# Attention and routed experts on one core: the leftover keys' value products as one group of four 64x64 tiles, heads swapped in half of the query tiles, queries split 256 and 320

## The chip, the core and the metric

One core of a Trainium2 chip runs one program. The metric is the device time of that program in microseconds (us). Its engines work side by side, each through its own list of instructions in order: TensorE (PE in the profile; PEld is its weight loads), VectorE (DVE), ScalarE (ACT), GpSimd (POOL) and SyncE (SP, which here only issues DMAs). Matrix products go from SBUF to PSUM, and DVE or ACT must copy them out of PSUM.

## The reference

```python
# q, k, v: 8 batches x 8 heads x 576 x 64, float32
scores = 1/sqrt(64) * q @ k.T
keep   = scores >= max(scores, -1) - tau
attn   = exp(scores - max) where keep, else 0;  attn /= sum(attn) + 1e-9
x      = (attn @ v), heads side by side           # 4608 x 512
logits = x @ w_gate                               # 4608 x 8, the router
# all 36864 (token, expert) pairs in descending order; a token goes to the first expert
# that still has room (576 tokens each); then per expert
out    = max(x @ w1[e], 0) @ w2[e]
```

## The kernel before

The first half of the program is attention (`attention`), the second the router and the experts (`moe`). The change is in attention and in the host's layout of q, k and v (`lay_qk`, `lay_v`).

**Pairs, tiles and slots.** Attention goes through 32 pairs of heads (pair p is batch p//4, heads 2j and 2j+1 with j = p%4). A pair has nine query tiles: tiles 0 to 7 are 128 queries of one head each (even ones the first head, odd ones the second), and tile 8 holds the last 64 queries of both heads, one head in each half of the partitions. There are 288 tiles, and the main loop (`for s_ in range(...)`) takes two of them per turn, in four steps that belong to different tiles. I call a turn a slot; a pair has 4.5 slots. In a slot PE writes the scores of two tiles into two `sc` tiles (`score`); DVE reads each `sc`, scales it into `z` and finds the maximum (`mx`); ACT takes the exponential of `z` into `pp` (tiles 0 to 7) or `pm` (tile 8) (`ex`); DVE applies the threshold and sums for the two tiles of the slot before (`stt`); PE transposes the weights of two older tiles into a `tb` bank (`tr`), and ACT copies the `tb` of the slot before into `pt` (`trev`). There are two `sc` tiles, one pair of `tb` banks and two `xo` banks in PSUM.

**Keys: 512 and 64 left over.** The 576 keys are four blocks of 128 and 64 left over. The four blocks are transposed by `tr`. For the left over, the first head's last 64 keys and the second head's first 64 keys lie side by side in memory (a `pp` tile holds both heads, 2 x 576 wide), so that one transposition of 128 columns takes both: `left` writes them into unused columns of the two `sc` tiles of that slot, and `leftev` has ACT copy them into `pl`. For tile 8 the second head's keys are stored rolled by 64 (`ke`), so that its leftover columns are in the same place as the first head's, and POOL copies 64 columns of `pm` once more.

**The value products.** `pv_unit(p,f,u)` multiplies key block u with queries of half f (288 each) for both heads: two matmuls of 128 rows and 64 columns side by side in the array. I call it a unit. Four units fill a bank `xo`; `pl_unit(p,f)` adds the leftover keys, again as two matmuls of 128 rows and 64 columns: 128 rows of `pl` hold both heads' leftover keys, and the values of the other head are stored as zeros. Then ACT copies `xo` into `xt`. So a pair has eight `pv` units and two `pl` units.

**Order.** Nothing is reordered at run time: the Python loop sets each engine's list. Units wait in `queue`, and `columns` takes as many per slot as `credit` allows (`RATE` is added per slot: two values, the second while work of the finished batch waits in `aux`). What a unit leaves to be copied out is put into `later` and written at the next `flush`. The slot writes in this order: scores and leftover transpositions on PE; `flush`; the `pt` copies; `flush`; `leftev`; `mx`, `ex`, `stt`; units; `aux` work (`whole`: gate logits `lg_unit`, their transposes, rows of x); transposes. In a slot in which `leftev` is due the first `flush` is left out. One rule breaks this order, because there are two `pt` buffers:

```python
while i==0 and p>1 and (p-2,"pv") not in have: st["credit"]=9; columns(); flush()
```

It stands ahead of the `pt` copy of a pair's tile 0. If the pair two before has not had its last unit, that unit is written now, on PE, and its copies to `xt` on ACT. For even p, tile 8 of pair p and tile 0 of pair p+1 are in one slot.

The slot with `leftev` is the one that the prediction speaks of: I call it the leftover slot; there is one per pair. In it the next `z` must wait for `leftev`, because the transposed leftover keys stand in the bank of `sc` that `z` reads.

Of the kernel before, what the change touches and what calls it, by code (L numbers as in the profile page):

```python
# [18 lines left out]
S=576; D=64; HS=288; QK=3*HS+2*S  # L19
PPB=8; LTB=1; VTB=5; HOLD=1; CAPV=3.3; XW=520; RATE=(2.4,2.4); NBO=2; NDEF=4; XTB=4; XTY=1.05; XT0=2.0; XRB=2  # L20


def attention(ctx, tc, qk, vl, tau, wgd, xrows, xts, Lg, nb_batches, ident, swap, R, after_first):
# [14 lines left out]
    def load(p):  # L38
        b,j=divmod(p,4)
        x=ld.tile([128,QK],F32,name="qk"); v=ld.tile([128,5,128],F32,name="vt",bufs=VTB)  # L40
        if p==0:

            a=HS+128; h=HS+S
            for q,c,e in ((nc.sync,0,a),(nc.scalar,h,h+a),(nc.sync,a,h),(nc.scalar,h+a,2*h),(nc.sync,2*h,QK)):
# [5 lines left out]
        for n,w in ((("k",0),HS),(("q",0),S),(("k",1),HS),(("q",1),S),(("ke",1),HS)):  # L50
            t[n]=x[:,c:c+w]; c+=w
        t["ke",0]=t["k",0]
        LD[p]=t
# [7 lines left out]
    def score(t):  # L61

        p,i=divmod(t,9); kd=LD[p]
        sc=ps_s.tile([128,2,512],F32,name="sc"); SC[t]=sc
        if i<8: todo=((i%2,"k",slice(0,128),slice(i//2*128,i//2*128+128)),)
        else: todo=((0,"ke",slice(0,64),slice(512,576)),(1,"ke",slice(64,128),slice(512,576)))
        for h,k,o,c in todo:
            for f in range(2):
                r=slice(64*f,64*f+64)
                T.matmul(sc[o,f,:HS], kd["q",h][r,c], kd[k,h][r,:],start=True,stop=True)  # L70
    ZB={}
    def mx(t):
        nb=wk.tile([128,2],F32,name="nb",bufs=6); NBI[t]=nb
        z=wk.tile([128,2,HS],F32,name="z",bufs=5); ZB[t]=z
        V.tensor_scalar(z,SC.pop(t)[:,:,:HS],-0.125,None,op0=ALU.mult,op1=ALU.min,accum_out=nb[:,0:1])  # L75
        G.tensor_scalar(nb[:,1:2],nb[:,0:1],taub[:,0:1],None,op0=ALU.add)  # L76
    def pview(t):
        p,i=divmod(t,9)
        if i==8:
            if t not in PB: PB[t]=wk.tile([128,S+D],F32,name="pm")  # L80
            return PB[t][:,:S]
        k=(p,i//2)
        if k not in PB: PB[k]=wk.tile([128,2,S],F32,name="pp",bufs=PPB)
        return PB[k][:,i%2]
    def ex(t):
        A.activation(pview(t),ZB[t].rearrange("p a b -> p (a b)"),AF.Exp,bias=NBI[t][:,0:1],scale=-1.0)  # L86
# [10 lines left out]
    def turn(o,x):  # L97
        for r in range(2):
            g=slice(64*r,64*r+64); T.transpose(o[:,r],x[g],ident[g,g])  # L99
# [4 lines left out]
    def tr(t,first):  # L104
        p,i=divmod(t,9)
        tb=bank(t,first)
        pv=pview(t)
        o=64 if (i<8 and i%2) else 0
        for kb in range(4): turn(tb[:,:,kb],pv[:,o+kb*128:o+(kb+1)*128])
# [8 lines left out]
    def left(p,n,t):  # L118
        sc=SC[t] if t is not None else ps_s.tile([128,2,512],F32,name="sc")
        LB[p,n]=sc  # L120
        for g in ((0,1,2),(3,))[n]: turn(sc[:,:,HS+64*(g%3):HS+64*(g%3)+64],PB[p,g].rearrange("p a b -> p (a b)")[:,512:640])
        if n: turn(sc[:,:,HS+64:HS+128],PB[p*9+8][:,512:640])
    def leftev(p):
        a=LB.pop((p,0)); b=LB.pop((p,1))
        A.activation(PL[p][:,0:384].rearrange("p (g r q) -> p r g q",g=3,r=2),a[:,:,HS:HS+192].rearrange("p r (g q) -> p r g q",g=3),AF.Copy)  # L125
        A.activation(PL[p][:,384:512].rearrange("p (r q) -> p r q",r=2),b[:,:,HS:HS+64],AF.Copy)
        for r in range(2): A.activation(PL[p][64*r:64*r+64,512:576],b[64*r:64*r+64,r,HS+64:HS+128],AF.Copy)
# [10 lines left out]
    def pv_unit(p,f,u):  # L138
        b,j=divmod(p,4)
        if b not in XT: XT[b]=wk.tile([128,4,S],F32,name="xt",bufs=XTB)  # L140
        if u==0: XO[p,f]=bank_v([128,512])
        xo=XO[p,f]; q=slice(f*HS,(f+1)*HS); v=LD[p]["v"]
        for h in range(2):
            T.matmul(xo[64*h:64*h+64,:HS],v[:,u,64*h:64*h+64],PT[p][:,h,u,q],start=(u==0),stop=False,skip_group_check=True)  # L144
    def pl_unit(p,f):
        b,j=divmod(p,4)
        q=slice(f*HS,(f+1)*HS); xo=XO.pop((p,f))
        for h in range(2):
            T.matmul(xo[64*h:64*h+64,:HS],LD[p]["v"][:,4,64*h:64*h+64],PL[p][:,q],start=False,stop=True,skip_group_check=True)  # L149
        if f==1: have[p,"pv"]=1  # L150
        return VB[id(xo)],lambda: A.activation(XT[b][:,j,q],xo[:,:HS],AF.Copy)  # L151
# [10 lines left out]
    def rd_unit(b):  # L162
        rd=RD[b]
        ps=bank_g(b,[128,512])
        T.matmul(ps[:,:4],swap,rd[:,:,8],start=True,stop=True)
        rm=wk.tile([128,4,2],F32,name="rm",bufs=XTB+NBO); RD["m",b]=rm
        def ev():
            V.tensor_copy(rm[0:64,:,0],rd[0:64,:,8]); V.tensor_copy(rm[64:128,:,1],rd[64:128,:,8])
            V.tensor_copy(rm[0:64,:,1],ps[0:64,:4]); V.tensor_copy(rm[64:128,:,0],ps[64:128,:4])
        return ev  # L170
    LT={}
    def lg_unit(b,f):
        if f==0: LT[b]=wk.tile([128,S+D],F32,name="lt",bufs=LTB)
        ps=bank_g(b,[128,512])
        for j in range(4):
            T.matmul(ps[32*j:32*j+32,:HS],wg[:,j],XT[b][:,j,f*HS:(f+1)*HS],start=True,stop=True,tile_position=(0,32*j))
        def ev():
            A.activation(LT[b][:,f*HS:(f+1)*HS],ps[:,:HS],AF.Copy)
            if f==1: G.tensor_scalar(LT[b][:,S:],LT[b][:,S-D:S],1.0,0.0,op0=ALU.mult,op1=ALU.add)
        return ev  # L180
# [42 lines left out]
    queue=[]; aux=[]; later=[]; late=[]; late2=[]; st={"last":-9,"slot":0,"credit":0.0}  # L223
    def push_pair(p):
        b,j=divmod(p,4)
        def when(n): return lambda: have.get((p,n),1<<30)+HOLD<=st["slot"]
        if p==NP-1:


            def left(f):  # L230
                k,g=pl_unit(p,f); g(); k[0]=True
# [3 lines left out]
            for g in (lambda: rd_unit(b)(),lambda: left(0),lambda: left(1),lambda: lg_unit(b,0)(),lambda: lg_unit(b,1)(),lambda: lgt_unit(b)(),lambda: lgm_unit(b)()):  # L235
                queue.append(("n",when("pl"),False,g))
            queue.append(("n",lambda: not later,False,lambda: late.extend([lambda c=c: xt_unit(b,c) for c in range(5)])))
            return
        for f in range(2):
            for u in range(4): queue.append(("c",when("t5" if f==0 else "t8"),u==0,lambda f=f,u=u: pv_unit(p,f,u)))  # L240
            if (f,j)==(0,3): queue.append(("n",when("t8"),False,lambda: rd_calc(b)))
            queue.append(("c",when("pl"),False,lambda f=f: pl_unit(p,f)))
# [3 lines left out]
    def finish(b):  # L246
        aux.extend([(0,lambda: rd_unit(b)),(0,lambda: lg_unit(b,0)),(0,lambda: lg_unit(b,1)),(1,lambda: lgt_unit(b)),(0,lambda: lgm_unit(b))])
# [8 lines left out]
    def columns():  # L256
        while queue and queue[0][1]():
            if queue[0][0]=="c":
                if st["credit"]<1 or (queue[0][2] and not free_v()): return
                st["credit"]-=1  # L260
            c,_,_,g=queue.pop(0); r=g()
            if c=="c" and r:
                later.append(r)
                if aux: return
    def whole():
        n=0
        while n<2 and aux and not XO and free_v() and st["slot"]>=st["last"]+aux[0][0]:
            r=aux.pop(0)[1](); n+=1; st["last"]=st["slot"]
# [11 lines left out]
    for s_ in range(-2,NT//2+2):  # L280
# [15 lines left out]
        for t in ev_:  # L296
            p,i=divmod(t,9)
            if i==5: push_pair(p)
# [582 lines left out]
def lay_qk(q,k):  # L881
# [3 lines left out]
    q=np.transpose(q,(0,1,3,2)); k=np.transpose(k,(0,1,3,2)); e=np.roll(k,-64,-1)  # L885
    for j in range(4):
        for f in range(2):
# [4 lines left out]
            o[:,j,f,:,c:]=e[:,2*j+1,:,f*HS:f*HS+HS]  # L892
    return o.reshape(B,4,128,QK)

def lay_v(v):


    B=v.shape[0]; o=np.zeros((B,4,128,5,128),v.dtype)
    for j in range(4):
        for h,o0 in ((0,0),(1,64)):  # L900
            o[:,j,:,0:4,64*h:64*h+64]=v[:,2*j+h,o0:o0+512].reshape(B,4,128,64).transpose(0,2,1,3)
        o[:,j,0:64,4,0:64]=v[:,2*j,512:576]; o[:,j,64:128,4,64:128]=v[:,2*j+1,0:64]
    return o
# [44 lines left out]
```

## Time and profile before

| | us |
|---|---|
| median of 3 runs (lowest, highest) | 1008.64 (1008.61, 1010.94) |
| the profiled execution: its time | 1010.9 |
| its span, first to last instruction | 1009.1 |
| attention, about | 5 to 487 |
| DVE busy between 20 and 480 | 430.38 of 460 |
| PE busy between 20 and 480 | 450.78 of 460 |
| ACT busy between 20 and 480 | 396.88 of 460 |

The time is some 2 us more than the span in the profiled execution, and that execution is the slow one of the three. In the rows of the profile `L75` is the `z` of `mx`, `L90` is `stt`, `L86` the exponential, `L70` the scores, `L99` all transposes inside attention (`tb` those of `tr`, `sc` those of `left`), `L114` and `L116` the `pt` copies, `L125` to `L127` `leftev`, `L144` the `pv` units, `L149` the `pl` units and `L151` their copies into `xt`. A PE instruction of this program is half of a float32 matmul, so a unit of two matmuls is four rows of the trace ("x4"). Instruction lengths overlap: a row's length is more than the distance to the next start.

### The profile page before, as it was taken

The page shows a single profiled execution, that of the slowest core. Times are in us where ns is not written, and L with a number is a line of the kernel's source. Part 1 is how long each engine was busy: PE and PEld are TensorE (multiplying, and loading weights), DVE is VectorE, ACT ScalarE, POOL GpSimd, SP SyncE. Part 2 cuts the span into 40 slices and gives each one's busy share as a digit, 9 for nine tenths or more (in the row PEclk, how much of TensorE's full clock was granted, in tenths as well). Part 3 has the DMA queues.
Part 4 walks back from the last instruction along what each step waited for, and adds up shares of the span by engine and source line. Part 5 has one row for each costly group of instructions (what it writes and reads, how often), then busy time and mean ns, then how long its engine had stood idle before and what let it go on. Part 6 is the DMA issues. An engine that isn't in the chain of part 4 may idle for free.

```text
span 1009.1 us, 24058 instructions
## 1 busy us (share of the span) xinstructions
PE 973.7 (96%) x9141; PEld 715.7 (71%) x9141; DVE 782.2 (78%) x2154; ACT 636.1 (63%) x1257; POOL 269.3 (27%) x443
## 2 busy tenths in 40 slices
PE   7999999999999999999879999999999999999996
PEld 4555555655655555555669789797887979899894
DVE  7999999999999999999578888788687787525220
ACT  6888888888888888888644344254342534545340
POOL 3333433333433343332020221212221203220202
PEclk9999999999999999999978999999999999999998
DMA  6322143243432133110771433434343415341101
GB/s 230 108 79 88 56 152 118 87 155 125 157 109 104 61 109 109 61 51 27 267 238 67 140 128 107 148 100 145 120 133 120 148 62 171 110 152 54 41 11 42
DMA packets 36004, 113.33 MB, mean 112 GB/s; under 512 B 4400, under 2 KB 5168, under 8 KB 35376
## 3 DMA queue, kind: packets, MB, share of 16 engines
q1 hardware_dynamic: 28496, 89.18, 25.1%
q0 software_dynamic: 5888, 19.03, 6.0%
q10 hardware_dynamic: 1504, 3.59, 1.1%
q8 instruction: 72, 1.18, 0.5%
q14 instruction: 44, 0.36, 0.1%
HBM read 89.34 MB, written 21.38 MB: 110 GB/s over the span
## 4 chain that ended last, share of the span: by engine, by line
PE 58%; DVE 19%; ACT 10%; issue 9%; DMA 2%; DVEq 0%; POOLq 0%; ACTq 0%
PE pf L781 21%; PE pf L813 19%; DVE z L75 7%; DVE pp L90 7%; ACT pp L86 5%; PE xo L144 5%; PE sc L70 4%; PE tb L99 3%; ACT pt L114 2%; PE pt L726 2%; ACT pt L116 1%; PE xo L205 1%; PE rps L434 1%; PE xo L149 1%; ACT pl L125 1%
## 5 line engine op out<-in xcount | busy, mean ns | idle before, releaser
L75 DVE TENSOR_SCALAR_CACHE_REDUCE z<-sc 128x576 f32<-128x576 f32 x288 | 205.8, 750 | 32.7 <-ACT pl L125 24.7
L76 POOL TENSOR_SCALAR nb<-nb,taub 128x1 f32<-128x1 f32 x288 | 146.5, 509 | 289.5 <-DVE z L75 255.9
L86 ACT ACTIVATE pp<-z,nb 128x576 f32<-128x576 f32 x256 | 187.7, 774 | 53.2 <-DVE z L75 52.5
L90 DVE SCALAR_TENSOR_TENSOR pp<-z,nb,pp 128x576 f32<-128x576 f32 x256 | 199.9, 812 | 0.3
L813 PE MATMUL pf<-w2h,H 128*128 128x512 f32 x576 | 195.1, 402 | 0.7 <-DVE H L366 0.7
L70 PE MATMUL sc<-qk 64*128 64x288 f32 (+1 forms) x1280 | 189.0, 432 | 2.6 <-DVE z L75 2.3
L144 PE MATMUL xo<-pt,vt 128*64 128x288 f32 x1024 | 151.7, 418 | 6.1 <-ACT xt L151 4.7
L114 ACT ACTIVATE pt<-tb 128x512 f32<-128x512 f32 x256 | 139.4, 591 | 8.8 <-PE tb L99 7.3
L813 PE MATMUL pf<-w2l,H 128*128 128x512 f32 x320 | 128.3, 401 | 0.0
L820 POOL DMA_INDIRECT out_dram<-y,idx x40 | 43.5, 1087 | 308.5 <-ACT y L816 248.9
L813 PEld LDWEIGHTS pf<-w2h,H 128*128 128x128 f32 x576 | 106.5, 189 | 20.0 <-DVE H L366 1.6
L70 PEld LDWEIGHTS sc<-qk 64*128 64x128 f32 (+1 forms) x1280 | 92.2, 180 | 30.2 <-DVE z L75 12.3
L144 PEld LDWEIGHTS xo<-pt,vt 128*64 128x64 f32 x1024 | 62.7, 136 | 70.3 <-issue 28.1
L99 PEld LDWEIGHTS tb<-ident,pp 64*128 64x128 f32 x2048 | 75.6, 139 | 50.9 <-issue 23.3
L781 PE MATMUL pf<-xh,w1h 128*128 128x288 f32 (+2 forms) x512 | 111.0, 303 | 0.7 <-ACT xh L727 0.7
L781 PE MATMUL pf<-xh,w1l 128*128 128x288 f32 (+2 forms) x512 | 110.6, 302 | 0.0
L781 PE MATMUL pf<-xl,w1h 128*128 128x288 f32 (+2 forms) x512 | 110.6, 302 | 0.0
L816 ACT ACTIVATE y<-pf 128x512 f32<-128x512 f32 x40 | 23.9, 598 | 127.0 <-PE pf L813 123.6
L99 PE MATMUL tb<-ident,pp 64*128 64x64 f32 x2048 | 94.3, 229 | 3.4 <-ACT pt L114 3.1
L793 ACT ACTIVATE hf<-pf 128x576 f32<-128x576 f32 x56 | 36.5, 653 | 89.5 <-PE pf L781 84.9
L781 PEld LDWEIGHTS pf<-xh,w1h 128*128 128x128 f32 x512 | 82.8, 192 | 1.5 <-ACT xh L727 1.1
L781 PEld LDWEIGHTS pf<-xh,w1l 128*128 128x128 f32 x512 | 82.6, 191 | 0.2
(199 smaller groups left out, 1358.4 us busy)
## 6 DMA issues: line engine op xcount, KB each, us to landing
qk<-qk_dram SPq DMA_DIRECT2D x31, 1008.0 KB, 5.0
w2s<-w_dram SPq DMA_DIRECT2D x32, 512.0 KB, 4.7
w1s<-w_dram SPq DMA_DIRECT2D x28, 512.0 KB, 5.2
vt<-vl_dram SPq DMA_DIRECT2D x32, 320.0 KB, 5.4
xrows<-pp SPq DMA_DIRECT2D x24, 260.0 KB, 2.3
xts<-xt SPq DMA_DIRECT2D x2, 1152.0 KB, 5.3
pt<-xts SPq DMA_DIRECT2D x2, 1152.0 KB, 7.5
xrows<-xr SPq DMA_DIRECT2D x8, 260.0 KB, 2.3
```

The source lines that it names most:

```text
L70: T.matmul(sc[o,f,:HS], kd["q",h][r,c], kd[k,h][r,:],start=True,stop=True)
L75: V.tensor_scalar(z,SC.pop(t)[:,:,:HS],-0.125,None,op0=ALU.mult,op1=ALU.min,accum_out=nb[:,0:1])
L76: G.tensor_scalar(nb[:,1:2],nb[:,0:1],taub[:,0:1],None,op0=ALU.add)
L86: A.activation(pview(t),ZB[t].rearrange("p a b -> p (a b)"),AF.Exp,bias=NBI[t][:,0:1],scale=-1.0)
L90: V.scalar_tensor_tensor(pv,ZB.pop(t).rearrange("p a b -> p (a b)"),NBI[t][:,1:2],pv,op0=ALU.is_le,op1=ALU.mult,accum_out=den_of(p)[:,p%4, ...
L99: g=slice(64*r,64*r+64); T.transpose(o[:,r],x[g],ident[g,g])
L114: A.activation(PT[p][:,i%2,:,(i//2)*128:(i//2+1)*128].rearrange("p k (r q) -> p r k q",r=2),tb,AF.Copy)
L144: T.matmul(xo[64*h:64*h+64,:HS],v[:,u,64*h:64*h+64],PT[p][:,h,u,q],start=(u==0),stop=False,skip_group_check=True)
L781: T.matmul(ps[:,h,:n],s[w][:,k,f*128:(f+1)*128],s[x][:,k,cols[h]],start=(i==0),stop=(i==11))
L793: A.activation(hf,ps[:,:,:HS],AF.Relu)
L813: T.matmul(ps[:,0,:],H[:,f,c:c+128],s[w][:,f],start=(f==0 and j==0),stop=e)
L820: G.indirect_dma_start(out=out,out_offset=IOA(ap=s["idx"][:n,t:t+1],axis=0),in_=y[:n],in_offset=None)
```

## The change

Per pair the leftover keys become one group. Queries are halved 256 and 320 (`FQ`) instead of 288 and 288. In query tiles 0 to 3 the first head's weights lie first in memory, as before; in tiles 4 to 7 the two heads change places (`place`), so that there the second head's last 64 keys and the first head's first 64 keys are left over. Then, for the two halves of the queries, the four products (head, half) use four different quarters of the array, each 64 rows by 64 columns, without the zeros. They are written one behind the other in one `pl_unit`, which therefore comes once a pair, when both `xo` banks are full; both banks stay open until then, and both copies to `xt` go into `later` together.

```diff
-S=576; D=64; HS=288; QK=3*HS+2*S
-PPB=8; LTB=1; VTB=5; ... RATE=(2.4,2.4); ...
+S=576; D=64; HS=288; QK=2*HS+2*S; FQ=(slice(0,256),slice(256,576))
+PPB=8; LTB=1; VTB=4; ... RATE=(2.02,2.6); ...
...
+    def place(i): return i%2 if i<4 else 1-i%2
+    PM=[cst.tile([128,S+2*D],F32,name="pm%d"%n) for n in range(2)]
+    for m in PM: V.memset(m[:,:D],0.0); V.memset(m[:,D+S:],0.0)
...
-        if i==8: G.tensor_scalar(PB[t][:,S:],PB[t][:,S-D:S],1.0,0.0,op0=ALU.mult,op1=ALU.add)
...
-    def pl_unit(p,f):
-        b,j=divmod(p,4)
-        q=slice(f*HS,(f+1)*HS); xo=XO.pop((p,f))
-        for h in range(2):
-            T.matmul(xo[64*h:64*h+64,:HS],LD[p]["v"][:,4,64*h:64*h+64],PL[p][:,q],start=False,stop=True,skip_group_check=True)
-        if f==1: have[p,"pv"]=1
-        return VB[id(xo)],lambda: A.activation(XT[b][:,j,q],xo[:,:HS],AF.Copy)
+    def pl_unit(p,fs=(0,1)):
+        b,j=divmod(p,4); r=[]
+        for f in fs:
+            xo=XO.pop((p,f)); q=FQ[f]; n=q.stop-q.start
+            for a in range(2):
+                g=slice(64*a,64*a+64); h=a^f
+                T.matmul(xo[64*h:64*h+64,:n],LD[p]["v"][g,f,512:576],PL[p][g,q],start=False,stop=True,skip_group_check=True)
+            r.append((VB[id(xo)],lambda xo=xo,q=q,n=n: A.activation(XT[b][:,j,q],xo[:,:n],AF.Copy)))
+        have[p,"pv"]=1
+        return r
...
-            for u in range(4): queue.append(("c",when("t5" if f==0 else "t8"),u==0,lambda f=f,u=u: pv_unit(p,f,u)))
+            for u in range(4): queue.append(("c",when("t3" if f==0 else "t8"),u==0,lambda f=f,u=u: pv_unit(p,f,u)))
...
-            queue.append(("c",when("pl"),False,lambda f=f: pl_unit(p,f)))
+        queue.append(("c",when("pl"),False,lambda: pl_unit(p)))
...
-                if st["credit"]<1 or (queue[0][2] and not free_v()): return
+                if st["credit"]<1 or (queue[0][2] and (not free_v() or (aux and not XO and st["held"]!=st["open"] and st["slot"]<NT//2))):
+                    return
```

What goes with it: the rolled keys `ke` are gone (`qk` per pair 864 KB instead of 1008), the values are stored once per half of the queries (`vt` 576 KB instead of 320, four buffers instead of five); tile 8 has two lasting buffers `pm0` and `pm1` with 64 zero columns at either end instead of POOL's copy; the reciprocals of tile 8 are swapped by a small matmul in the first gate unit's bank instead of in a bank of their own (`rd_unit` goes into `lg_unit`); the last pair keeps two separate `pl` groups. The experts are not touched. In the changed file the lines of attention are numbered a little differently: `z` is L74, the `pt` copies L113 and L115, `leftev` L124 to L126, `pv` L143, `pl` L151, the `xt` copies L152, transposes L98 and scores L69.

Two places of the lists, both in the leftover slot of pair 26 (the pairs 16, 18, 22 and 30 have the same). First ACT, before, from the `pt` copy of tile 8 (`L116`) on:

```order
L116 ACTIVATE pt<-tb 128x8x64
L114 ACTIVATE pt<-tb 128x2x4x64
L125 ACTIVATE pl<-sc 128x2x3x64
L126 ACTIVATE pl<-sc 128x128
L127 ACTIVATE pl<-sc 64x64 x2
L86 ACTIVATE pp<-z,nb 128x576 x2
```

The two `pt` copies are followed at once by `leftev`. The same place after the change:

```order
L115 ACTIVATE pt<-tb 128x8x64
L152 ACTIVATE xt<-xo 128x256
L152 ACTIVATE xt<-xo 128x320
L113 ACTIVATE pt<-tb 128x2x4x64
L124 ACTIVATE pl<-sc 128x2x3x64
L125 ACTIVATE pl<-sc 128x128
L126 ACTIVATE pl<-sc 64x64 x2
L86 ACTIVATE pp<-z,nb 128x576 x2
```

Both copies of the pair before (pair 25 of the list, whose `pt` buffer is wanted) now stand between the two `pt` copies, ahead of `leftev`. PE in the same slot, before, from the transposes of tile 8 on (`tb<-ident,pm`):

```order
L99 MATMUL tb<-ident,pm 128x64 x8
L99 MATMUL tb<-ident,pp 128x64 x8
L70 MATMUL sc<-qk 128x288 x2
L99 MATMUL sc<-ident,pp 128x64 x6
L70 MATMUL sc<-qk 128x288 x2
L99 MATMUL sc<-ident,pp 128x64 x2
L99 MATMUL sc<-ident,pm 128x64 x2
L144 MATMUL xo<-pt,vt 64x288 x4
L99 MATMUL tb<-ident,pp 128x64 x16
```

After two score tiles, each with its leftover transposes, come two units of the value products. After the change:

```order
L98 MATMUL tb<-ident,pm_100 128x64 x8
L98 MATMUL tb<-ident,pp 128x64 x8
L69 MATMUL sc<-qk 128x288 x2
L98 MATMUL sc<-ident,pp 128x64 x6
L69 MATMUL sc<-qk 128x288 x2
L98 MATMUL sc<-ident,pp 128x64 x2
L98 MATMUL sc<-ident,pm_100 128x64 x2
L143 MATMUL xo<-pt,vt 64x320 x2
L151 MATMUL xo<-pl,vt 64x256 x2
L151 MATMUL xo<-pl,vt 64x320 x2
L143 MATMUL xo<-pt,vt 64x256 x6
L98 MATMUL tb<-ident,pp 128x64 x16
```

The last unit and the leftover group of the pair before, whose copies ACT writes ahead of `leftev`, stand here behind all score tiles and leftover transposes of the slot.

More of the change, by code (lines that the diff above doesn't have):

```diff
@@ L107, in tr @@
         pv=pview(t)
-        o=64 if (i<8 and i%2) else 0
-        for kb in range(4): turn(tb[:,:,kb],pv[:,o+kb*128:o+(kb+1)*128])
+        o=(64,0) if i==8 else (64*place(i),)*2
+        for kb in range(4): turn(tb[:,:,kb],*(pv[:,c+kb*128:c+(kb+1)*128] for c in o))
     def trev(t):
@@ L217, in xt_unit @@
         return ev
-    queue=[]; aux=[]; later=[]; late=[]; late2=[]; st={"last":-9,"slot":0,"credit":0.0}
+    queue=[]; aux=[]; later=[]; late=[]; late2=[]; st={"last":-9,"slot":0,"credit":0.0,"held":-1,"open":0}
     def push_pair(p):
```

88 lines of the change are left out of this document (42 added, 46 removed).

## The prediction

> **What bounds attention.** First the busy time of each engine between 20 and 480 us (columns: PE, PEld, DVE, ACT, POOL; clock, DMA share, GB/s), then the waits on DVE in that stretch (us in total, times, longest).
>
> ```profile
> 20.00:480.00 460.00, 450.78 (x5265) 265.07 (x5267) 430.38 (x1233) 396.88 (x766) 164.29 (x330) 1.00 0.28 98
> ```
>
> ```profile
> DVE z L75 <- ACT pl L125: 24.7, 30, 1.3
> DVE z L75 <- PE sc L70: 1.8, 4, 1.0
> ```
>
> By busy time PE (98%) is the engine in demand, DVE (94%) comes next. But DVE loses 29.6 us, and 24.7 of them in 30 waits of one kind: `z` waits for the first copy of `leftev`. It hardly ever waits for PE. The DVE timeline shows the beat (start, length, engine, line):
>
> ```profile
> 202.55 0.76 DVE L75 TENSOR_SCALAR_CACHE_REDUCE z<-sc 128x576 f32<-128x576 f32 x1 [0.72 <-ACT pl L125]
> ...
> 205.40 0.75 DVE L75 TENSOR_SCALAR_CACHE_REDUCE z<-sc 128x576 f32<-128x576 f32 x1
> ...
> 375.57 0.75 DVE L75 TENSOR_SCALAR_CACHE_REDUCE z<-sc 128x576 f32<-128x576 f32 x1
> ...
> 376.25 0.75 DVE L75 TENSOR_SCALAR_CACHE_REDUCE z<-sc 128x576 f32<-128x576 f32 x1
> ...
> 379.20 0.76 DVE L75 TENSOR_SCALAR_CACHE_REDUCE z<-sc 128x576 f32<-128x576 f32 x1 [0.72 <-ACT pl L125]
> ...
> 422.41 0.76 DVE L75 TENSOR_SCALAR_CACHE_REDUCE z<-sc 128x576 f32<-128x576 f32 x1 [1.02 <-ACT pl L125]
> ...
> 451.43 0.76 DVE L75 TENSOR_SCALAR_CACHE_REDUCE z<-sc 128x576 f32<-128x576 f32 x1 [1.32 <-ACT pl L125]
> ```
>
> From the first `z` of a slot to the first of the next it is 2.85 us (202.55 to 205.40): two `z` and two `stt` without a gap. Into a leftover slot it is 3.63 (375.57 to 379.20). The wait there has three sizes, 0.72, 1.02 and 1.32: with none, one and two copies out of `xo` ahead of `leftev` in ACT's list, 0.30 each. So the quantity to forecast is what stands ahead of `leftev` on ACT, and when it can run. The slot that ends at 379.20, on ACT and on PE:
>
> ```profile
> 376.36 1.45 ACT L86 ACTIVATE pp<-z,nb 128x576 f32<-128x576 f32 x2
> 377.72 0.58 ACT L116 ACTIVATE pt<-tb 128x512 f32<-128x512 f32 x1
> 378.20 0.59 ACT L114 ACTIVATE pt<-tb 128x512 f32<-128x512 f32 x1
> 378.68 0.49 ACT L125 ACTIVATE pl<-sc 128x384 f32<-128x384 f32 x1
> ```
>
> ```profile
> 377.74 0.70 PE L70 MATMUL sc<-qk 64*128 64x288 f32 x4
> 378.27 0.22 PE L99 MATMUL sc<-ident,pp 64*128 64x64 f32 x2
> 378.33 0.23 PE L99 MATMUL sc<-ident,pm 64*128 64x64 f32 x2
> 378.49 1.19 PE L144 MATMUL xo<-pt,vt 128*64 128x288 f32 x8
> ```
>
> ACT runs without a break: exponentials, two `pt` copies 0.48 apart, `leftev`; `z` follows 0.52 after `leftev` starts. PE is not in this chain: it comes to its value products at 378.49, 2.92 after the slot's first `z`, and nobody waits for them.
>
> **Leftover slots after the change.** I count from the two lists what lies ahead of `leftev` in the 31 leftover slots that a `z` follows. Now: in 13 nothing; in 8 two `xt` copies behind both `pt` copies, of products that PE wrote a slot earlier; in 1 two gate copies; in 9 (pairs 8, 10, 12, 14, 16, 18, 22, 26, 30) the two `xt` copies between the `pt` copies, of a leftover group that PE is given only in this slot, behind all scores and leftover transposes. The first three kinds have prices above: 13 x 0.72 = 9.4, 9 x 1.32 = 11.9.
>
> The nine forced ones are new: ACT, and behind it `leftev` and `z`, waits for PE. No row shows this, so I build it. PE can start the group where it now starts the units, 2.92 after the slot's first `z`. Its own length, and how soon ACT follows:
>
> ```profile
> 203.38 1.39 PE L70 MATMUL sc<-qk 64*128 64x288 f32 x12
> 204.71 0.71 PE L149 MATMUL xo<-pl,vt 128*64 128x288 f32 x4
> 205.34 0.66 PE L205 MATMUL xo<-ident,xt 128*128 128x128 f32 x4
> ...
> 208.05 1.68 PE L144 MATMUL xo<-pt,vt 128*64 128x288 f32 x12 [0.34 <-ACT xt L151]
> ...
> 210.21 1.19 PE L70 MATMUL sc<-qk 64*128 64x288 f32 x8
> 211.33 0.71 PE L144 MATMUL xo<-pt,vt 128*64 128x288 f32 x4
> ```
>
> ```profile
> 482.09 1.19 PE L149 MATMUL xo<-pl,vt 128*64 128x288 f32 x8
> ```
>
> ```profile
> 482.85 0.90 ACT L151 ACTIVATE xt<-xo 128x288 f32<-128x288 f32 x2 [3.05 <-PE xo L149]
> ```
>
> A unit of 288 columns adds 0.49 (x8 1.19 in the next fence, x12 1.68), by columns 0.43 for 256 and 0.54 for 320; alone it takes 0.63 until the next work starts (204.71 to 205.34), so a run of another shape costs 0.14 to 0.15. The x12 at 203.38 holds four matmuls of 64x64 for tile 8 in place of two of 64x128: 1.33 to the next start against 1.12 for the plain x8, 0.21 more for the changes of shape and nothing more for four quarters at once. So the new group should take 0.54, and 0.76 from start to result (0.71 for 288); ACT follows 0.05 later (482.09 + 0.71 = 482.80, 482.85). Then from the slot's first `z`: 2.92 + 0.76 + 0.05 = 3.73; two copies 0.60 and one `pt` copy 0.48 bring `leftev` to 4.81 and `z` to 5.33, against 3.63: 1.70 more, a wait of 2.42. So in the four slots where the group stands first (pairs 8 to 14). In the other five a unit of 320 stands ahead of it, with a change of shape: 0.54 + 0.15 = 0.69 more, a wait of 3.11. Together 4 x 2.42 + 5 x 3.11 = 25.2.
>
> The ends of the 2.92: the second score tile cannot start before the second `z` has read its bank (376.25 + 0.75 = 377.00), and from that tile to the units it is 0.75 (377.74 to 378.49): 2.18. On the other side a slot in which PE was behind:
>
> ```profile
> 405.44 0.75 DVE L75 TENSOR_SCALAR_CACHE_REDUCE z<-sc 128x576 f32<-128x576 f32 x1
> ```
>
> ```profile
> 408.93 1.19 PE L144 MATMUL xo<-pt,vt 128*64 128x288 f32 x8
> ```
>
> That is 3.49. I take the middle row, 2.92; the ends move nine slots by -0.74 or +0.57: -6.7 or +5.1.
>
> **Sum of the leftover slots:** 9.4 + 11.9 + 25.2 = 46.5, less 24.7 now: +21.8 us. DVE has no free time to give it back: in the other slots it runs without a gap.
>
> **The other parts.** PE: per pair two `pl` units of 0.49 become one group of 0.54, 31 x 0.44 = 13.6 saved; changes of shape fall from 379 to 369 by my count, 1.5 more. This PE time is off the path; it can only take away the 1.8 us that `z` waits for scores. I take -1.5; slots with three units of 320 columns (1.62 against 1.46) could put some back. The gain of 0 elsewhere is covered by DVE's 2.85 per slot, and without that cover it would be 15. Opening a bank: both are open until the group, so the next pair's first unit waits for an `xt` copy (0.34 at 208.05 before); nobody but the transposes stands behind it. POOL loses 32 small copies, at 36% busy. DMA: 1440 KB a pair instead of 1328 at a share of 0.28, through SP's list in unchanged order and asked for more than a slot ahead: 0 (it would be the extra 112 KB, under 1 us a pair at the 98 GB/s of this stretch, if nothing covered it). The start:
>
> ```profile
> 1.59 0.11 DVE L271 MEMSET idle<- 128x64 uint32 x1
> ```
>
> ```profile
> 1.76 2.10 PE L278 MATMUL xo<-idle 128*128 128x128 bf16 x18 [1.76 <-DVE idle L271]
> 4.08 2.29 PE L70 MATMUL sc<-qk 64*128 64x288 f32 x8 [0.22 <-DMA qk<-qk_dram]
> ```
>
> Four fills of zeros at 0.11 stand ahead of the one that the warm-up matmuls need; these end 0.22 ahead of the first scores, so 0.44 - 0.22 = 0.2. The end (last pair: same columns, two groups of two quarters, one change of shape more) I take as 0.1. The experts are unchanged and move along whole.
>
> Sum: 21.8 - 1.5 + 0.3 = +20.6, call it +20. The profiled execution took 1010.9, so it would take 1031; it is 2.3 above the median. Against the median: 1008.6 + 20 = **1028.6 us**. Its own range: -6.7 and -2 for stalls that also vanish gives 1020; +5.1 and +2 for the long slots gives 1036.
>
> **Rivals.** (a) *PE is the bound, and the saving counts.* For it: 98% busy, four quarters at once. Then 1008.6 - 15.1 = 993.5. Against it: waits of DVE for PE are 1.8 us in all, and slots without `leftev` are exactly DVE's length. It decides only if the beat of 2.85 were set by PE. By the Trainium skill, "TensorEngine Tiling (Array Packing)", section "Theoretical Speedup", a dimension of at most 64 brings a factor of 2, so halved leftover products (0.97 to 0.49 a pair) would give 31 x 0.48 = 14.9 us, about the same time; the x12 row agrees on the factor. By the skill's "Perfetto Trace Analysis", section "Identifying the Most-Contended Engine", matmul busy time is no measure of how close PE is to its limit, and for VectorE busy time is a fair one: by that rule DVE's 94% counts and (a) falls. Chance 0.05.
>
> (b) *ACT's waits shrink, a little faster.* If the forced copies came off their place (the group done before ACT has finished the first `pt` copy, 2.63 after the first `z`) and all leftover slots cost 0.72: 31 x 0.72 = 22.3, less 24.7, less 1.8: -4, 1004.5. The sign changes where the nine forced slots cost under (24.7 + 1.2 - 9.4 - 11.9) / 9 = 0.5 each. Against it: the earliest group ends at 2.18 + 0.76 = 2.94. Chance 0.05.
>
> (c) *The forced slots cost no more than two copies,* 9 x 1.32 = 11.9 in place of 25.2: +6.7, 1015. It would need PE to run ahead of the second `z`, which only another bank of `sc` would allow. Chance 0.09.
>
> (d) *The change does not do what it says on PE:* the four quarters run one after the other or in two pairs. Then every group takes 0.5 to 1.6 longer, which counts in the nine slots: 5 to 14 more, 1034 to 1043. Against it: the x12 row. Chance 0.06.
>
> **Chances.** The forecast has 0.75, of which 0.03 lie above 1036. Range 1014 to 1036: it leaves out (a), (b), most of (d) and that edge, about 0.18. Changes within 0.3% (3 us), about what a measurement of this kernel can tell from none, come from (b) and the gap between (b) and (c): 0.04. Faster 0.07, slower 0.89.
>
> **What would show it.** In the profile of the changed kernel: the wait of `z` for L124 at some 45 us, in nine slots above 2 us, the five later ones longest; ACT idle ahead of L152 for PE in those nine; slots without `leftev` still at 2.85; PE's time on L151 about half of L149's, with more idle time on PE; the experts' length unchanged. The forecast is wrong if the nine slots show L152 ready when ACT comes to it, or if slots of 2.85 become shorter.

## The result and the profile after

The changed kernel takes 1026.69 us (median of 4 runs, 1025.84 to 1028.29) against 1008.77 for the kernel before in the same comparison (4 runs, 1008.61 to 1010.94): a ratio of 1.0174, 95% interval 1.0155 to 1.0194. It is slower, and the forecast of 1028.6 lies 1.9 above the time. The profiled execution took 1026.09, its span is 1024.3.

First the busy time of each engine between 20 and 480 us (columns as before: PE, PEld, DVE, ACT, POOL; clock, DMA share, GB/s), then the waits of DVE and of ACT between 20 and 490 us (us in total, times, longest).

```profile
20.00:480.00 460.00, 427.13 (x5063) 246.59 (x5061) 415.31 (x1193) 381.24 (x736) 150.23 (x292) 1.00 0.30 103
```

```profile
DVE z L74 <- ACT pl L124: 45.1, 31, 3.5
```

```profile
ACT xt L152 <- PE xo L151: 10.8, 9, 1.4
```

PE has 23.7 us less to do in this stretch than before, since it does less work per pair and gets through fewer pairs, and DVE, which had 430.38, has 415.31: it stands still for longer. Nearly all of its idle time is one wait, `z` for the first copy of `leftev`: 45.1 us instead of 24.7. The wait of `z` for scores (1.8 before) is gone. And ACT now waits nine times for the leftover group on PE ahead of an `xt` copy, which it did only once before, for the last pair (3.05 at 482.85). The difference is 20.4 - 1.8 = 18.6 us; from the third slot's first `z` to the last slot's, the trace shows 18.3. Before, on DVE:

```profile
11.77 0.75 DVE L75 TENSOR_SCALAR_CACHE_REDUCE z<-sc 128x576 f32<-128x576 f32 x1
...
470.64 0.75 DVE L75 TENSOR_SCALAR_CACHE_REDUCE z<-sc 128x576 f32<-128x576 f32 x1
```

After, with the ends of a leftover slot of the cheap kind (406.05) and of a forced one (424.86) between:

```profile
10.74 0.75 DVE L74 TENSOR_SCALAR_CACHE_REDUCE z<-sc 128x576 f32<-128x576 f32 x1
...
406.05 0.76 DVE L74 TENSOR_SCALAR_CACHE_REDUCE z<-sc 128x576 f32<-128x576 f32 x1 [0.72 <-ACT pl L124]
...
419.26 0.75 DVE L74 TENSOR_SCALAR_CACHE_REDUCE z<-sc 128x576 f32<-128x576 f32 x1
...
424.86 0.76 DVE L74 TENSOR_SCALAR_CACHE_REDUCE z<-sc 128x576 f32<-128x576 f32 x1 [2.69 <-ACT pl L124]
...
487.91 0.75 DVE L74 TENSOR_SCALAR_CACHE_REDUCE z<-sc 128x576 f32<-128x576 f32 x1
```

470.64 - 11.77 = 458.9 before, 487.91 - 10.74 = 477.2 after. I call this stretch the loop time; it holds nothing of the start or of the experts. DVE is busy for 430.29 of the 458.87 and for 429.79 of the 477.16: its work in the loop is the same, and the whole difference is time in which it stands still. The slot from 419.26 to 424.86 is the one whose lists stand under the change (pair 26). ACT and PE in it:

```profile
420.05 1.45 ACT L86 ACTIVATE pp<-z,nb 128x576 f32<-128x576 f32 x2 [0.41 <-DVE z L74]
421.41 0.58 ACT L115 ACTIVATE pt<-tb 128x512 f32<-128x512 f32 x1
423.24 0.71 ACT L152 ACTIVATE xt<-xo 128x256 f32<-128x256 f32 x2 [1.25 <-PE xo L151]
423.84 0.60 ACT L113 ACTIVATE pt<-tb 128x512 f32<-128x512 f32 x1
424.32 0.51 ACT L124 ACTIVATE pl<-sc 128x384 f32<-128x384 f32 x1
```

```profile
421.70 0.23 PE L98 MATMUL sc<-ident,pm 64*128 64x64 f32 x2
421.86 0.76 PE L143 MATMUL xo<-pt,vt 128*64 128x320 f32 x4
422.55 0.77 PE L151 MATMUL xo<-pl,vt 64*64 64x256 f32 x8
```

Read from right to left: `z` starts 0.54 after `leftev`; `leftev` stands behind a `pt` copy (0.48) and two `xt` copies (0.60); these wait 1.25 for PE, which does the unit of 320 and the group only behind all scores and transposes of the slot. Eight rows of the group run in 0.77, where four rows of one old `pl` unit took 0.71: the four quarters do work side by side. To the next start on PE a group takes 0.70 to 0.77, the two old units of a pair 0.54 to 0.71 each, some 1.2 together.

### The profile page after: what moved, and what is told of

The parts are those of the page before. It is cut to its first block, busy times and chain, and to the rows that moved or that the text cites. A ratio compares the mean times of both kernels' runs of the same rounds, so it can differ in the third digit from the quotient of the medians.

```text
span 1024.3 us, 24024 instructions
## 1 busy us (share of the span) xinstructions
PE 962.7 (94%) x9141; PEld 703.2 (69%) x9141; DVE 781.3 (76%) x2158; ACT 633.5 (62%) x1257; POOL 259.5 (25%) x411
## 4 chain that ended last, share of the span: by engine, by line
PE 62%; DVE 15%; ACT 11%; issue 9%; DMA 2%; DVEq 0%; POOL 0%; POOLq 0%; ACTq 0%
PE pf L781 21%; PE pf L813 18%; PE xo L143 7%; DVE z L74 6%; PE sc L69 5%; DVE pp L90 5%; ACT pp L86 4%; PE tb L98 3%; ACT pt L113 3%; ACT xt L152 2%; PE pt L726 2%; ACT pl L124 1%; PE rps L434 1%; ACT pt L115 1%; PE xo L204 1%
## 5 line engine op out<-in xcount | busy, mean ns | idle before, releaser
L74 DVE TENSOR_SCALAR_CACHE_REDUCE z<-sc 128x576 f32<-128x576 f32 x288 | 205.4, 749 | 49.9 <-ACT pl L124 45.1
L75 POOL TENSOR_SCALAR nb<-nb,taub 128x1 f32<-128x1 f32 x288 | 150.7, 523 | 325.4 <-DVE z L74 294.9
L69 PE MATMUL sc<-qk 64*128 64x288 f32 (+1 forms) x1280 | 190.6, 432 | 5.2 <-DVE z L74 5.1
L143 PE MATMUL xo<-pt,vt 128*64 128x320 f32 (+1 forms) x1024 | 148.4, 416 | 15.9 <-DVE xr L212 5.4
L113 ACT ACTIVATE pt<-tb 128x512 f32<-128x512 f32 x256 | 139.0, 590 | 2.2 <-PE tb L98 1.9
L143 PEld LDWEIGHTS xo<-pt,vt 128*64 128x64 f32 x1024 | 64.7, 136 | 82.7 <-issue 31.0
L98 PEld LDWEIGHTS tb<-ident,pp 64*128 64x128 f32 x2048 | 75.0, 138 | 63.3 <-ACT pt L113 34.9
L69 PEld LDWEIGHTS sc<-qk 64*128 64x128 f32 (+1 forms) x1280 | 88.6, 177 | 38.3 <-DVE z L74 26.3
L98 PE MATMUL tb<-ident,pp 64*128 64x64 f32 x2048 | 94.0, 229 | 7.9 <-ACT pt L113 7.4
```

The costliest lines, as they stand in the source:

```text
L69: T.matmul(sc[o,f,:HS], kd["q",h][r,c], kd["k",h][r,:],start=True,stop=True)
L98: g=slice(64*r,64*r+64); T.transpose(o[:,r],x[r%len(x)][g],ident[g,g])
L113: A.activation(PT[p][:,i%2,:,(i//2)*128:(i//2+1)*128].rearrange("p k (r q) -> p r k q",r=2),tb,AF.Copy)
L143: T.matmul(xo[64*h:64*h+64,:q.stop-q.start],v[:,f,128*u+64*h:128*u+64*h+64],PT[p][:,h,u,q],start=(u==0),stop=False,skip_group_check=True)
```

## The experiments

Twelve kernels ran, on four chips on which the kernel before took 1013.7 to 1015.7; so times are compared as ratios to it, each taken on one chip, with the loop time of the profiled execution beside them. The two need not agree to better than some 4 us (run 4: 1.2% less is 12 us, and its loop time is 8.0 less): the rest of the span, start and experts, varies from 547 to 558 us between these profiles. In the loop DVE is busy for 427 to 431 us in every run but run 11 (435), so loop times differ by how long DVE stands still. "Forced" is a leftover slot in which the rule for the `pt` buffers puts `xt` copies between the two `pt` copies, by the lists.

| run | edit | ratio, 95% interval | loop time | to before |
|---|---|---|---|---|
| - | before | 1 | 458.9 | 0 |
| - | the change | 1.0174 (1.0155 to 1.0194) | 477.2 | +18.3 |
| 1 | change, `xt` copies behind `leftev` | 1.0137 (1.0108 to 1.0166) | 474.7 | +15.8 |
| 2 | change, only units forced | 1.0103 (1.0076 to 1.0130) | 470.3 | +11.4 |
| 3 | before, `xt` copies behind `leftev` | 1.0009 (0.9993 to 1.0025) | 462.0 | +3.1 |
| 4 | change, RATE (2.2,3.0) | 0.9880 (0.9848 to 0.9913) | 450.9 | -8.0 |
| 5 | change, RATE (2.2,2.6) | 1.0083 (1.0053 to 1.0113) | 470.6 | +11.7 |
| 6 | run 4, group twice | 1.0020 (1.0000 to 1.0040) | 462.9 | +4.0 |
| 7 | change, two groups, RATE (2.4,2.4) | 1.0004 (0.9986 to 1.0023) | 462.0 | +3.1 |
| 8 | before, RATE (2.0,2.0) | 1.0122 (1.0089 to 1.0154) | 470.2 | +11.3 |
| 9 | change, group twice | 1.0232 (1.0193 to 1.0271) | 481.6 | +22.7 |
| 10 | before, RATE (2.4,3.0) | 1.0044 (1.0025 to 1.0064) | 462.8 | +3.9 |
| 11 | run 4, `leftev` split | 1.0149 (1.0116 to 1.0182) | 474.5 | +15.6 |
| 12 | change, RATE (2.02,3.0) | 0.9954 (0.9936 to 0.9971) | 455.7 | -3.2 |

**Runs 1 and 3: only the place of the copies on ACT.** In a leftover slot all `xt` copies are written behind `leftev`, in the changed kernel and in the one before.

```diff
-            while i==0 and p>1 and (p-2,"pv") not in have: st["credit"]=9; columns(); flush()
+            while i==0 and p>1 and (p-2,"pv") not in have:
+                st["credit"]=9; columns()
+                if (p-2,"pv") not in have: flush()
             trev(t); have[p,f"t{i}"]=s_
-        flush()
+        if not p8 or ev_[-1]==NT-1: flush()
...
-            if i==8: leftev(p); have[p,"pl"]=s_
+            if i==8:
+                leftev(p); have[p,"pl"]=s_
+                flush()
```

> The changed kernel, with one thing moved: in a leftover slot the copies out of xo are written on ACT behind leftev, where the changed kernel writes them between or behind the two pt copies. PE's list stays as it is, the nine forced groups too. Theory (the nine forced slots cost because leftev, and with it the next z, stands on ACT behind two copies that wait for PE): the waits of z for L124 fall from 45.1 us to 26 x 0.72 + 5 x 1.5 = 26, the five being pairs 16, 18, 22, 26 and 30, where a pt copy must itself still wait for a unit of 320 on PE; so 19 us less, 1026.7 - 19 = 1008 (1005 to 1011). Rival A (PE is late by the group itself, or PE's work is the bound): PE's list has not changed, so the time stays at 1026.7. Rival B (the copies are merely moved and cost the same 0.60 behind leftev, since ACT has no free time): 9 x 0.6 + 10 x 0.6 come back one slot later, about 1015 to 1020.

> The kernel before with the same move as the first run: copies out of xo in a leftover slot are written behind leftev. Theory: its 22 copies ahead of leftev cost it what lies above 0.72 in its waits: 24.7 - 31 x 0.72 = 2.4 us, so 1006.4 (1005 to 1008). Rival (ACT's full list gives it back in the next slot): 1008.8.

Both expectations of my theory failed. The waits behind `leftev` fall, by 13 us (I had expected 19) and by 6 us, but most or all of it comes back. Waits of DVE in run 1, then in run 3:

```profile
DVE z L74 <- ACT pl L124: 32.1, 30, 1.6
DVE z L74 <- PE sc L69: 8.1, 17, 1.7
```

```profile
DVE z L75 <- ACT pl L125: 19.0, 28, 0.8
DVE z L75 <- PE sc L70: 9.5, 13, 1.0
```

The new wait for scores has its cause on PE. In run 1, the group of a forced slot, and what stands behind it on PE; then DVE in the next slot:

```profile
297.15 0.77 PE L151 MATMUL xo<-pl,vt 64*64 64x256 f32 x8
299.25 1.52 PE L143 MATMUL xo<-pt,vt 128*64 128x256 f32 x12 [1.33 <-ACT xt L152]
```

```profile
302.01 0.76 DVE L74 TENSOR_SCALAR_CACHE_REDUCE z<-sc 128x576 f32<-128x576 f32 x1 [0.74 <-PE sc L69]
```

The copies are also what frees the `xo` banks. Moved behind `leftev`, they hold up the next pair's first unit (1.33 here, 0.36 at the same kind of place in the changed kernel), and the transposes and the scores of the next slot stand behind that unit on PE. In all PE waits 23.3 us for `L152` in run 1 against 12.8 in the changed kernel. For run 1, rival B, which gave the copies back one slot later, came nearest, and yet no outcome that I had named was right: its 1015 to 1020 is a ratio of 1.006 to 1.011, and 1.0137 lies between that and the unchanged time. For run 3 the rival, nothing gained, was right. Their reason, ACT's full list, is not what the trace shows. So of the 18 us that the change loses, moving the copies on ACT alone gives back 2.5.

**Run 2: no forced group, only forced units.**

```diff
-            while i==0 and p>1 and (p-2,"pv") not in have: st["credit"]=9; columns(); flush()
+            c0=st["credit"]
+            while i==0 and p>1 and (p-2,"u") not in have: st["credit"]=1; columns()
+            st["credit"]=c0
```

(`have[p,"u"]` is set with the last `pv` unit, and `pl` is claimed in `leftev`.)

> The changed kernel with the rule's condition loosened: ahead of tile 0 only the units that read the pt buffer are forced (the last unit of 320), not the group of leftover keys, which reads pl; pl is claimed only in leftev. Copies out of xo stay where the changed kernel has them, but none is forced between the pt copies any more: 29 leftover slots have no copy ahead of leftev, 3 have two. Theory (the forced copies on ACT): 24 x 0.72 + 5 x 1.5 (a pt copy still waits for the forced unit of 320) + 2 x 1.2 = 27, against 45.1: 18 less, 1009 (1005 to 1012). Rival A (PE is the bound): the same matmuls in nearly the same order, 1026.7. Rival B (the forced unit on PE is what costs, not the copies): the five slots of pairs 16 to 30 keep their 2.7, only the four of pairs 8 to 14 fall: 1018.

It gives 7 us, not 18. Rival B's time (1018, a ratio of 1.009) lies in the interval, but its picture holds only in part: the five slots of pairs 16 to 30 keep waits of 2.07 to 2.58, but of the four of pairs 8 to 14 only that of pair 8 falls, and the others keep 2.50 to 3.34. ACT does not wait for the group any more, but longer for the units. A wait of ACT, and PE in the slot that ends with it:

```profile
ACT pt L113 <- PE xo L144: 15.0, 8, 2.5
```

```profile
298.21 1.84 PE L144 MATMUL xo<-pt,vt 128*64 128x320 f32 x12
299.98 0.77 PE L153 MATMUL xo<-pl,vt 64*64 64x256 f32 x8
```

Three units of 320 (x12), not one, stand ahead of the `pt` copy, because the forced slot no longer gives credit and the units fall further behind. By this run, what matters is that the units of pair p-2 are not done when pair p wants their `pt` buffer; which of their products is forced is secondary. Since the run changes the credit as well, it does not show this by itself. A third `pt` buffer would test it directly and was not tried.

**Runs 4, 5 and 12: the pace alone.** `RATE` is what a slot adds to `credit`, the second number while gate work waits in `aux`. The change brought (2.02,2.6).

```diff
-... RATE=(2.02,2.6); ...
+... RATE=(2.2,3.0); ...
```

(run 5: (2.2,2.6); run 12: (2.02,3.0))

> The changed kernel with other pace numbers alone, RATE=(2.2,3.0) for (2.02,2.6). By the lists no leftover slot is forced any more: 28 have nothing ahead of leftev, 4 have two copies. Theory (the cost came through the forced slots, which the pace numbers and the later group bring about, not through four quarters or longer units): waits of 27 x 0.72 + 4 x 1.32 = 24.7, 20 us less than the changed kernel, 1006.5 (1004 to 1010). Rival A (the group of four quarters, the halves of 256 and 320 or the larger vt transfer cost by themselves): 1015 or more. Rival B (PE is the bound): 1026.7, since PE's work is the same.

> The changed kernel with RATE=(2.2,2.6): only the first of the two pace numbers of the fourth run, the second as in the changed kernel. By the lists 5 leftover slots are still forced, and 38 copies instead of 6 stand ahead of leftev. Theory (what counts is whether units keep pace while gate work waits, the second number): priced as the fourth run's and the changed kernel's own slots were (0.8 without a copy, 0.3 a copy, 2.7 forced, less DVE's own extra work in the slot) the stall is 40 us, against 48 in the changed kernel and 20 in the fourth run: 8 us less than the changed kernel, a ratio to the kernel before of 1.010 (1.006 to 1.014). Rival A (the first number brings the gain): the stall of the fourth run, 0.988 to 0.992. Rival B (neither; the fourth run was fast for some other reason): 1.017.

> The changed kernel with RATE=(2.02,3.0): only the second pace number of the fourth run, the first as in the changed kernel; with the fifth run this completes the square of the two numbers. By the lists no leftover slot is forced, 20 copies stand ahead of leftev (the fourth run has 6, the changed kernel 38). Theory (the pace while gate work waits decides whether slots are forced; the first number only spares single copies): priced as before, 21.3 us of stall against 18.4 in the fourth run by the same count, so 3 us more than the fourth run: a ratio of 0.991 (0.987 to 0.995). Rival (both numbers are needed, since 2.02 x 4.5 slots give just the nine units of a pair): 1.005 or more.

Run 4 is faster than both kernels and than the 1004 to 1010 that I had expected (1006.5 is a ratio of 0.998): 26 us less loop time than the changed kernel with the same group, halves, loads and number of matmuls. Run 5 came as expected. Of the two numbers the second does most of it: 477.2 with (2.02,2.6), 470.6 with the first alone raised, 455.7 with the second alone, 450.9 with both. Run 12 came with the sign that I expected, a little above its range (0.9954; 0.987 to 0.995): its loop time is 4.8 above run 4's, not 3. By the order on PE, while gate work waits, 2.6 lets PE write 3, 2 and 3 units and puts the group into a fourth slot, which is forced (the group of pairs 7, 9, 11 and 13); in pairs 15, 17, 21, 25 and 29 it is 3, 2, 2, and 1 with the group. With 3.0 the first four write 3, 3, and 2 with the group, in three slots. The other five write 3, 2, 2, and 1 with the group as before, but begin two slots earlier, because the pair ahead of them is done earlier. So in run 4 each of the nine groups is written two or three slots ahead of the slot in which its `pt` buffer is wanted: no slot is forced. Run 4's waits, and one leftover slot of it on ACT and DVE:

```profile
DVE z L74 <- ACT pl L124: 15.6, 22, 1.1
DVE z L74 <- PE sc L69: 3.3, 6, 0.7
```

```profile
126.05 0.52 ACT L124 ACTIVATE pl<-sc 128x384 f32<-128x384 f32 x1
```

```profile
125.75 1.28 DVE L212 COPY xr<-xo 128x512 f32<-128x512 f32 x2
126.95 0.75 DVE L74 TENSOR_SCALAR_CACHE_REDUCE z<-sc 128x576 f32<-128x576 f32 x1
```

22 waits instead of 31, since in nine leftover slots DVE has rows of x or gate work to copy at that very time, as here: `leftev` started at 126.05, DVE was busy until 126.95, and `z` waits for nothing. That is the main reason why run 4 came out below the 24.7 of waits that I had expected (15.6), a gain I had not foreseen.

**Runs 7 and 8: the group without forced slots, forced slots without the group.** Run 7 closes each half of the queries with a group of two quarters of its own, like the kernel before, and runs at its pace; run 8 is the kernel before, slowed until its rule bites.

```diff
 # run 7
-        queue.append(("c",when("pl"),False,lambda: pl_unit(p)))
+            queue.append(("c",when("pl"),False,lambda f=f: pl_unit(p,(f,))))
 # run 8, in the kernel before
-... RATE=(2.4,2.4); ...
+... RATE=(2.0,2.0); ...
```

> The changed kernel with the leftover products in two groups of two quarters, one behind the units of each half of the queries, as the kernel before has its two pl units; RATE=(2.4,2.4) as before. Halves of 256 and 320, head places and all else as changed. No leftover slot is forced by the lists, 27 copies ahead of leftev, stall by the same prices 28.4 us against 27.8 in the kernel before. Theory (the loss comes from closing both halves at once at a pace that is too slow, not from quarters, halves or loads): a ratio of 1.000 (0.996 to 1.004). Rival (quarters, longer units or the larger vt load cost by themselves): 1.008 or more.

> The kernel before with one edit, RATE=(2.0,2.0) for (2.4,2.4): a pair has ten units and 4.5 slots give only 9, so by the lists 14 of its leftover slots become forced, each with one pl unit of 288 on PE and one xt copy between the pt copies; nothing of the 64x64 group is in it. Theory (a forced slot costs what PE's late product, the copy and the pt copy behind it take): 14 x 1.9 + 3 x 1.1 + 14 x 0.8 = 41 us of stall against 27.8: +13, a ratio of 1.013 (1.009 to 1.020). Rival A (forced slots cost only by the new group): +1, 1.001. Rival B (the slower pace spares PE and is a gain): below 0.998.

Both came as the theory had it. 64x64 quarters, halves of 256 and 320, places and the larger `vt` together cost nothing that run 7 tells from zero (1.0004). On PE run 7 has the layout without the saving: its two groups a pair take 0.54 to 0.69 each to the next start, the two old units 0.54 to 0.71. And the kernel before, without any of them, loses 1.22% as soon as its leftover slots are forced. ACT, PE and DVE there, in one of the 14:

```profile
417.74 0.41 ACT L151 ACTIVATE xt<-xo 128x288 f32<-128x288 f32 x1 [1.43 <-PE xo L149]
```

```profile
416.99 0.71 PE L149 MATMUL xo<-pl,vt 128*64 128x288 f32 x4
```

```profile
419.05 0.76 DVE L75 TENSOR_SCALAR_CACHE_REDUCE z<-sc 128x576 f32<-128x576 f32 x1 [2.61 <-ACT pl L125]
```

The 14 waits lie between 1.52 and 2.61 and sum to 28.3, 2.0 each, with one product of 288 and one copy; I had expected 1.9.

**Runs 9 and 6: what PE's time is worth.** The matmuls of every leftover group are issued twice, in the changed kernel (run 9) and in run 4 (run 6).

```diff
-            for a in range(2):
+            for a in (0,1)*(2 if len(fs)==2 else 1):
```

> The changed kernel, its pace numbers untouched, with the matmuls of every leftover group issued twice (the output holds that product twice): 31 x 0.57 = 17.7 us more on PE. It measures what the saved PE time was worth in the changed kernel itself. Theory (PE's time counts only where ACT waits for a late product): 9 x 0.57 = 5 in the forced slots, and 2 to 6 in slots where the group stands with other units; 7 to 11 us more than the changed kernel, a ratio to before of 1.026 (1.022 to 1.029). Rival A (PE's time is wholly off the path outside the forced slots): 5 us, 1.022. Rival B (PE bounds, as in 12 of 17 us it seemed to in the sixth run): 17.7 us, 1.035.

> The fourth run's kernel (RATE=(2.2,3.0)) with the matmuls of every leftover group issued twice (the output holds that product twice): 31 x 0.54 = 17 us more work on PE, whose load per pair is then about that of the kernel before. Theory (DVE with its waits for ACT bounds; PE's saving lies off the path, and so does its return): 0 to 4 us more than the fourth run, in slots in which PE was just in time; a ratio of 0.988 to 0.992. Rival (PE is the bound, and the fourth run is faster than before because it has less PE work): 17 us more, 1.005.

On PE a doubled group takes 1.25 to the next start instead of 0.70, so the edit adds some 17 us (31 x 0.55; I had taken 0.57). In the changed kernel 4.4 of them come through (481.6 - 477.2): the wait of `z` behind `leftev` rises from 45.1 to 49.3, 3.9 of that in the nine forced slots, 0.43 each; elsewhere PE's work is covered. My theory had 7 to 11; it is rival A, the forced slots alone, that the loop time bears out, and the ratio tells the two apart badly (1.0232; 1.022 for rival A, 1.022 to 1.029 for the theory).

```profile
DVE z L74 <- ACT pl L124: 49.3, 31, 3.9
```

In run 4 the same edit costs 12.0 (462.9 - 450.9), where I had expected 0 to 4; the rival, 17 us, was nearer. Waits of DVE in run 6:

```profile
DVE z L74 <- ACT pl L124: 16.9, 22, 1.1
DVE z L74 <- PE sc L69: 12.2, 24, 1.3
```

And the busy time of run 4 between 20 and 460 us:

```profile
20.00:460.00 440.00, 429.27 (x5133) 251.28 (x5129) 418.94 (x1204) 383.55 (x747) 154.09 (x294) 1.00 0.32 108
```

The wait for scores rises from 3.3 to 12.2. At this pace PE is busy for 98% (429.27 of 440; 93% in the changed kernel), a slot can hold two units of 320 and a group, and PE reaches the next scores just in time or late. So added PE time counts for a quarter of itself at the slow pace (4.4 of 17) and for some seven tenths at the fast one (12.0 of 17); with the group doubled, run 4's lead of 8.0 over the kernel before is gone.

**Run 10: the faster pace without the change.** The kernel before with RATE=(2.4,3.0).

> The kernel before with RATE=(2.4,3.0): the second pace number raised as in the fourth run, nothing else. It tells whether the fourth run is faster than the kernel before by its pace alone. By the lists the same 20 copies stand ahead of leftev and no x rows fall into leftover slots; only three units of a slot are spread a little otherwise. Theory (the fourth run's 8 us come from copies gone from ahead of leftev and from DVE's x rows falling into leftover slots, which takes one group a pair): 0 to 3 us less, a ratio of 0.997 to 1.000. Rival (pace alone): 0.988 to 0.992.

It is 0.4% slower, where I had expected 0 to 0.3% faster; pace alone is no gain. Run 4 needs both.

**Run 11: `leftev` in two parts,** in run 4.

```diff
+    def leftev0(p):
+        a=LB.pop((p,0))
+        A.activation(PL[p][:,0:384]...,a[:,:,HS:HS+192]...,AF.Copy)
...
-        for t in sc_:
+        for n,t in enumerate(sc_):
             mx(t)
             ex(t)
+            if n==1:
+                for p in p8: leftev0(p)
```

> The fourth run's kernel with leftev in two parts: the copies out of the second score bank stay where leftev stood, the copy of 384 columns out of the first bank (0.37 to the next start) comes behind both exponentials. The first z then waits for no copy, the second for the smaller ones. Theory (what is left of the stall is z behind leftev): the second z waits some 0.3 where the first waited 0.8, 22 slots: 5 to 11 us less, a ratio of 0.978 to 0.984. Rival (the first bank comes free 0.4 later for the next scores, PE waits in order, and units behind the scores slip): nothing gained or up to 5 us lost, 0.988 to 0.993.

The rival was right and too mild. The waits of `z`:

```profile
DVE z L74 <- PE sc L69: 21.3, 42, 0.9
DVE z L74 <- ACT pl L125: 11.4, 21, 0.7
```

PE's wait for the copy that was moved (`L130`):

```profile
PE sc L69 <- ACT pl L130: 12.9, 30, 0.4
```

The wait behind `leftev` falls from 15.6 to 11.4, but the first score bank is free later: PE waits 30 times for the moved copy before it can write scores, and `z` waits 42 times for scores, 21.3 us against 3.3 in run 4. Run 4 stays the best kernel found.

## Why the prediction was right, and where not

**What bounds.** Right for the changed kernel: the loop time is DVE's own work (a plain slot takes 2.84 after, 2.85 before; with rows of x and gate work 429.8 in all) and the leftover waits, and run 9 shows rival (a) false there. By the Trainium skill, "Perfetto Trace Analysis", section "Identifying the Most-Contended Engine", matmul busy time tells little of how near PE is to its limit. The trace agrees: with PE at 427 of 460 us, 17 us more matmuls cost 4.4. But the rule must not be read as "PE has room": in run 6 they cost 12.0.

**The sum of the leftover slots.** Forecast 46.5, measured 45.1. The two parts:

- Forced slots: forecast 25.2, measured 24.45 (2.52, 3.51, 2.52 and 2.72 for the pairs with the group first, 2.43 and four times 2.68 or 2.69 for those with a unit ahead). Rivals (b) and (c) fall by these waits: all nine are above 1.32. The total is right in part by luck, because two terms were off against each other. With the group first I took 2.42 and the mean is 2.82, since the group started 3.06 to 3.32 after the slot's first `z` in three of these slots, not 2.92, and 4.11 after it in the slot of 3.51. There PE came to the transposes late, and ACT waited for them too:

```profile
173.57 0.60 ACT L115 ACTIVATE pt<-tb 128x512 f32<-128x512 f32 x1 [0.59 <-PE tb L98]
175.54 0.71 ACT L152 ACTIVATE xt<-xo 128x256 f32<-128x256 f32 x2 [1.37 <-PE xo L151]
```

  With a unit ahead I took 3.11 and it is 2.69: PE was there 2.60 after the slot's first `z` (421.86 - 419.26), not 2.92; in pair 16, with 2.43, it was there after 2.29. The step that failed is this one start on PE, taken from a single slot; its stated ends, 2.18 and 3.49, held in eight of the nine slots, and the ninth was 4.11.
- The others: forecast 21.3, measured 20.7 in 22 waits. The three sizes behind that forecast (0.72, 1.02, 1.32) are those of 17 of the 30 waits before; the other 13 lie between 0.41 and 0.82.

**The group's length.** Taken as 0.54, and 0.76 to the result: 422.55 to 423.24, when ACT goes on, is 0.69, where the forecast had 0.81 with the 0.05 for ACT; by the code the first copy needs only the half of 256, which is written first. Rival (d) falls.

**The other parts.** The wait for scores fell by 1.8 (I took 1.5). The start was forecast 0.2 late; the warm-up matmuls do start 0.30 later (2.06 against 1.76) and the first `z` 0.07 later (5.53 against 5.46), but the third slot's first `z` is 1.0 earlier (10.74 against 11.77). One execution can't test a term of 0.2 there: in the profiles of the runs that `z` lies between 10.57 and 12.14 with the changed layout, and between 11.22 and 12.26 in the kernel before and its edits. The larger loads were put at 0, and in this stretch no engine waits for a DMA; the bound given for them was too low, since 112 KB at 98 GB/s is 1.1 us, not under 1. The time was 1.9 below the forecast.

**What the prediction did not see.** It priced the nine forced slots and took them as given by the list; runs 4 and 12 show that they hang on one number of the change, the pace while gate work waits. And it named what stands ahead of `leftev` as the quantity to forecast. That is good for reading a wait, but it is no remedy: runs 1, 3 and 11 moved copies on ACT and lost on PE most of what they gained, or more.

## What to carry to other kernels

A wait behind a copy tells where the time shows, not what to move: ask what else that copy releases, here a PSUM bank for which PE stands in line with the next scores behind it. When a change makes work cheaper but joins it into one later step, look at the pace that feeds that step; if the step comes too late for a buffer, its price is the whole chain behind the buffer (waits of 2.0 us on average in run 8 and 2.7 in the changed kernel, against 0.72 in a slot without copies, for 0.5 and 0.7 us of matmuls). And test a saving on an engine that seems idle by doubling that work: 4.4 of 17 us at one pace and 12.0 at another is the answer that busy shares (93 and 98%) do not give.

## What I had not expected

DVE's row copies hide the leftover wait completely where they fall into the same slot: nine of 31 waits were gone in run 4 without any instruction less. And a copy of 0.37 us out of a score bank, moved behind two exponentials, brought 42 waits for scores, 21.3 us in all, where run 4 has 6 and 3.3 (run 11): here the bank's release counted for more than the copy's own time.
